# Moving the `wo` loads of a decode kernel behind its last K tile, with contiguous rows for the other weights

## Chip, cores, metric

The kernel runs on one core of a Trainium2 chip. The metric is the device time of one execution in microseconds (us), which includes about 1.8 us around the span that the profile shows.

## The reference, cut to what matters

One decode step for 8 sequences (B = 8, one token each, D = 512): grouped attention over a window of 2048 cached tokens (8 KV heads of 128, 32 query heads), the output projection `wo`, then a small MLP with `w3` (512 × 1792) and `w4` (1792 × 512). The token shift branch (`w1`, `w2`) is identically zero at sequence length 1.

```python
q = (layernorm(x) @ wq)                       # wq 512 x 4096, 4.19 MB
p = softmax(q k[-2048:] / sqrt(128)); o = p v  # K and V: 64 tiles each of 2048 x 128 bf16, 67.1 MB
h = x + o @ wo                                 # wo 4096 x 512, 4.19 MB
xb = layernorm(h)
h2 = gelu(layernorm(xb) @ w3) @ w4             # w3, w4: 1.84 MB each
out = h + xb + h2
```

Everything is bf16 and each byte is used once per step, so loading 79.2 MB is most of the work.

## The kernel before

An item i is one (sequence, KV head) pair, i = 0 to 63; a batch is the 8 items of one sequence. For each K tile the TensorE makes 16 transposes (`pe_T`) and 4 score matmuls. After each batch come softmax and 128 P·V matmuls, with V tiles of 512 KB. All loads are issued from one engine.

```python
def sp_prog(e):                                # the load program, in order
    e.dma_start(x_sb, A_x)
    for kc in range(KC):                       # KC = 4
        e.dma_start(wq_v[:, kc, :], A_wq[kc*128:(kc+1)*128, :]).then_inc(sem_wq, 16)
    for i in range(NITEM):
        ...                                    # wait for a free K slot (15 of them)
        e.dma_start(knat[:, ks, :], K tile i).then_inc(sem_k[ks], 16)
        while v_next <= i - VD and v_next < V_DEFER_FROM:    # V follows K by 5; V56..63 wait
            issue_v(v_next); v_next += 1
        for _ in range(2):                     # from item 12 on: two 128 KB pieces of wo per K
            if i >= W_START and wi < len(wdmas): ...
    ...
    while v_next < NITEM: issue_v(v_next); v_next += 1       # V56..63
    e.wait_ge(sem_Thi, W34_LAST_ITEM + 1)      # w3 and w4 reuse K slots
    for dst, src, wsem in w34dmas:             # 4 pieces of w3, 14 of w4, one semaphore
        e.dma_start(dst, src).then_inc(wsem, 16)
...
def pe_attn(e):                                # the wo product
    e.wait_ge(sem_oT, NB)
    e.wait_ge(sem_wo, 16 * N_WO)
    for h in range(H): ...                     # 32 matmuls, 4 column tiles
...
def pe_h3(e):                                  # the w3 product
    e.wait_ge(sem_w34, 16 * N_W34)
    for fc in range(FC):                       # FC = 14
        for kc in range(KC):
            e.matmul(misc[...], w3_sb[:, kc, fc*128:(fc+1)*128], uT[:, kc*B:(kc+1)*B], ...)
...
def pe_h2(e): ...                              # the w4 product, 14 matmuls
```

## Time and profile before

| | before |
|---|---|
| time, first measurement | 214.96 us (214.67 to 216.75, 3 runs) |
| span of the profiled run | 213.3 us |
| last landings: wq, K63, V63, wo, w3/w4 | 13.5, 178.2, 188.3, 89.5, 197.5 us |
| wo product, w3 product | 193.9 to 197.5, 204.0 to 205.6 us |

The landing times here and below are read from the trace: the moment when the semaphore of a load got its sixteenth increment.

These are rows of the page's slices for the kernel before, each digit or number one fortieth of the span (5.3 us): TensorE busy tenths, granted TensorE clock in tenths, busy tenths of the DMA engines, and GB/s.

```profile
...
PE   1049955998389956799769987798899589788143
...
PEclk9999999967859696795998599769966995785855
DMA  6999999999999999999999999999999999996000
GB/s 198 420 422 416 420 415 420 406 411 411 403 416 409 406 408 409 415 415 418 420 416 421 415 415 423 416 416 418 416 416 421 416 419 418 414 398 206 0 3 2
...
```

The DMA row is full and the GB/s flat from the second slice to the end of the loads. The TensorE row has holes. So the stream of bytes is the limit, and the TensorE waits for it. The waits say the same; this is the line of the view of who waited for whom, with us in total, times and the longest:

```profile
...
PE kT_ps L397 <- DMA knat<-in_A_k_cache_dram: 25.6, 28, 2.0
...
```

The chain that ended last, in order of time (start, us, what), for the kernel before:

```profile
...
156.76 16.51 DMA knat<-in_A_k_cache_dram
...
173.32 1.07 PE kT_ps L397 x16
...
193.88 3.62 PE S_ps L587 x32
...
203.96 1.67 PE misc L671 x56
...
```

The last load that this chain names is K60, which landed at 173.3 us. No load of a weight stands after it: `wo` had landed 104 us before its use, and `w3`/`w4` 6.5 us before theirs. The timeline (start, us, engine, line, what, count, and in brackets what ended the idle time before) shows the end of the kernel as a string of dependent steps:

```profile
...
188.71 1.74 PE L535 MATMUL misc<-pT_sb,vnat 128*128 128x4 bf16 x64 [0.44 <-DVE pT_sb L494]
...
190.96 1.86 PE L535 MATMUL misc<-pT_sb,vnat 128*128 128x4 bf16 x64
...
193.88 3.58 PE L587 MATMUL S_ps<-wbig,oT_all 128*8 128x512 bf16 x32 [1.06 <-DVE oT_all L549]
...
198.26 0.38 PE L604 MATMUL misc<-C_sb,sel_b 128*8 128x512 bf16 x1 [0.80 <-DVE C_sb L597]
...
198.57 0.37 PE L605 MATMUL misc<-x_sb,ident_b 8*8 8x512 bf16 x1
...
203.96 1.66 PE L671 MATMUL misc<-uT,knat 128*128 128x8 bf16 x56 [0.41 <-DVE uT L660]
...
207.57 1.87 PE L716 MATMUL S_ps<-knat,gT 128*8 128x512 bf16 x14 [1.95 <-DVE gT L705]
...
```

L535 is P·V of the last batch, L587 the wo product, L604 and L605 the two matmuls that sum it, L671 the w3 product, L716 the w4 product. The groups by shape give the w3 product and its weight loads (busy us, mean ns of one):

```profile
...
L671 PE MATMUL misc<-uT,knat 128*128 128x8 bf16 x56 | 1.7, 168 | 0.4 <-DVE uT L660 0.4
L671 PEld LDWEIGHTS misc<-uT,knat 128*128 128x128 bf16 x56 | 1.6, 104 | 0.5 <-DVE uT L660 0.5
...
```

And the view of stretches gives the granted clock (column PEclk) between the wo and w3 products, and in the w3 product:

```profile
...
core 0: us, PE busy (x) PEld busy (x) DVE busy (x) ACT busy (x) POOL busy (x), PEclk, DMA share, GB/s
...
197.60:203.20 5.60, 0.68 (x2) 0.16 (x2) 3.93 (x10) 1.30 (x3) 0.00 (x0) 0.79 0.00 0
203.90:205.70 1.80, 1.66 (x56) 1.57 (x56) 0.05 (x2) 0.00 (x0) 0.00 (x0) 0.50 0.03 9
...
```

### The profile page before, as it was taken

The numbers are of one execution on the slowest core, as the hardware profiler recorded it, in microseconds if no ns is written. First come the engines' busy times: TensorE is split into PE (matmuls) and PEld (weight loads), VectorE is DVE, ScalarE is ACT, GpSimd is POOL, SyncE is SP. The second block draws the span as 40 slices with busy tenths as digits, with TensorE's granted clock in tenths as the row PEclk, the third lists the DMA queues.
The fourth block names the chain that finished last, engine by engine and source line by source line (L and its number), as shares of the span: only waits on it lengthen the run. The fifth ranks groups of instructions, "written<-read, shape, count | busy, mean of one in ns | idle before, by whom it ended". The sixth has DMA issues, their size and how long they took to land.

```text
span 213.3 us, 6096 instructions
## 1 busy us (share of the span) xinstructions
PE 160.1 (75%) x2627; PEld 119.7 (56%) x2627; DVE 88.9 (42%) x205; ACT 81.5 (38%) x98; POOL 2.8 (1%) x11
## 2 busy tenths in 40 slices
PE   1049955998389956799769987798899589788143
PEld 0049734786267734487548764776687368563030
DVE  6104534532425332534453456147533553441652
ACT  3204748314352333413551365047515541340120
POOL 5000000000000000000000000000000000000000
PEclk9999999967859696795998599769966995785855
DMA  6999999999999999999999999999999999996000
GB/s 198 420 422 416 420 415 420 406 411 411 403 416 409 406 408 409 415 415 418 420 416 421 415 415 423 416 416 418 416 416 421 416 419 418 414 398 206 0 3 2
DMA packets 26265, 79.57 MB, mean 373 GB/s; under 512 B 2928, under 2 KB 8832, under 8 KB 25728
## 3 DMA queue, kind: packets, MB, share of 16 engines
q1 hardware_dynamic: 26240, 79.20, 92.6%
q8 instruction: 21, 0.34, 0.6%
q14 instruction: 4, 0.03, 0.0%
HBM read 79.18 MB, written 0.01 MB: 371 GB/s over the span
## 4 chain that ended last, share of the span: by engine, by line
DMA 40%; SPq 34%; PE 17%; DVE 5%; issue 3%; ACT 1%; DVEq 0%
DMA knat<-in_A_k_cache_dram 40%; SPq L247 13%; SPq L237 12%; SPq L259 8%; PE kT_ps L397 6%; PE misc L535 5%; PE S_ps L587 2%; PE S_ps L427 1%; SPq L228 1%; PE S_ps L716 1%; PE misc L671 1%; PE b L516 1%; DVE st L279 1%; DVE xb_f L292 0%; ACT P_sb L448 0%
## 5 line engine op out<-in xcount | busy, mean ns | idle before, releaser
L397 PE MATMUL kT_ps<-ident_b,knat 128*128 128x128 bf16 x1024 | 85.5, 251 | 25.7 <-DMA knat<-in_A_k_cache_dram 25.6
L408 ACT ACTIVATE kT_sb<-kT_ps 128x1024 bf16<-128x1024 bf16 x64 | 65.5, 1024 | 94.2 <-PE kT_ps L397 94.1
L397 PEld LDWEIGHTS kT_ps<-ident_b,knat 128*128 128x128 bf16 x1024 | 73.4, 114 | 43.2 <-DMA knat<-in_A_k_cache_dram 35.6
L415 DVE COPY kT_sb<-kT_ps 128x1024 bf16<-128x1024 bf16 x64 | 44.3, 692 | 69.0 <-PE kT_ps L397 68.5
L535 PE MATMUL misc<-pT_sb,vnat 128*128 128x4 bf16 x1024 | 28.7, 165 | 1.5 <-issue 1.1
L535 PEld LDWEIGHTS misc<-pT_sb,vnat 128*128 128x128 bf16 x1024 | 27.3, 98 | 4.5 <-issue 3.0
L427 PE MATMUL S_ps<-kT_sb,qblk 128*32 128x512 bf16 x256 | 29.5, 445 | 0.3 <-DVE kT_sb L415 0.3
L427 PEld LDWEIGHTS S_ps<-kT_sb,qblk 128*32 128x32 bf16 x256 | 6.7, 95 | 9.4 <-issue 4.0
L448 ACT ACTIVATE P_sb<-S_ps,negmcol 128x512 bf16<-128x512 f32 x8 | 5.5, 688 | 7.7 <-DVE negmcol L440 7.6
L369 PE MATMUL S_ps<-xlnT,wbig 128*128 128x8 bf16 x128 | 3.6, 168 | 6.1 <-DMA wbig<-in_A_wq_dram 6.1
L521 DVE COPY w_sb<-b 128x128 f32<-128x128 f32 x8 | 2.3, 292 | 13.5 <-PE b L516 13.5
L545 DVE TENSOR_TENSOR prod_sb<-misc,w_sb 128x128 f32<-128x128 f32 x8 | 2.3, 292 | 13.0 <-PE misc L535 13.0
L369 PEld LDWEIGHTS S_ps<-xlnT,wbig 128*128 128x128 bf16 x128 | 3.5, 104 | 6.2 <-issue 6.2
L438 DVE TENSOR_REDUCE mcol<-S_ps 128x1 f32<-128x512 f32 x8 | 5.5, 682 | 0.6 <-PE S_ps L427 0.6
L285 ACT ACTIVATE stdv<-mv,eps_t 8x1 f32<-8x1 f32 x3 | 0.9, 294 | 12.5 <-DVE mv L281 12.5
L385 DVE TENSOR_SCALAR qblk<-S_ps 128x32 bf16<-128x32 f32 x8 | 0.9, 182 | 9.5 <-PE S_ps L369 9.5
L587 PE MATMUL S_ps<-wbig,oT_all 128*8 128x512 bf16 x32 | 3.6, 627 | 1.1 <-DVE oT_all L549 1.1
L455 PE MATMUL misc<-ident_f,mcol 128*1 128x128 f32 x16 | 3.6, 309 | 1.0 <-DVE negmcol L440 1.0
L472 ACT ACTIVATE a_row<-d_row 1x128 f32<-1x128 f32 x8 | 2.5, 306 | 4.7 <-DVE d_row L465 4.6
L516 PE MATMUL b<-w_row,ones_row 1*128 1x128 f32 x16 | 4.0, 334 | 0.0
L285 ACT ACT_TABLE_LOAD x2 | 2.6, 1283 | 2.8 <-DVE mv L281 2.8
L494 DVE COPY pT_sb<-b 128x512 bf16<-128x512 bf16 x8 | 3.4, 426 | 0.4 <-PE b L482 0.2
(74 smaller groups left out, 66.0 us busy)
## 6 DMA issues: line engine op xcount, KB each, us to landing
knat<-in_A_k_cache_dram SPq DMA_DIRECT2D x64, 512.0 KB, 14.9
vnat<-in_A_v_cache_dram SPq DMA_DIRECT2D x64, 512.0 KB, 14.9
wbig<-in_A_wq_dram SPq DMA_DIRECT2D x4, 1024.0 KB, 8.0
wbig<-in_A_wo_dram SPq DMA_DIRECT2D x32, 128.0 KB, 9.8
knat<-in_B_w_dram SPq DMA_DIRECT2D x4, 448.0 KB, 12.8
knat<-in_B_w_dram SPq DMA_DIRECT2D x14, 128.0 KB, 6.0
x_sb<-in_A_x_dram SPq DMA_DIRECT2D x1, 8.0 KB
out_dram<-out_sb SPq DMA_DIRECT2D x1, 8.0 KB
```

The lines of the kernel that those rows point to most:

```text
L237: e.dma_start(vnat[:, vs, :].rearrange("p (c d) -> p c d", c=NC), A_v_cache[b, g, W0:SK, :].rearrange("(p c) d -> p c d", c=NC),).then_inc ...
L247: e.dma_start(knat[:, ks, :].rearrange("p (c d) -> p c d", c=NC), A_k_cache[b, g, W0:SK, :].rearrange("(p c) d -> p c d", c=NC),).then_inc ...
L259: e.dma_start(dst, src).then_inc(wsem, 16)
L369: ins = e.matmul(S_ps[:, 0, h * B:(h + 1) * B], wq_v[:, kc, h * DH:(h + 1) * DH], xlnT[:, kc * B:(kc + 1) * B], start=(kc == 0), stop=(kc ...
L397: ins = e.matmul(buf[:, c * 128:(c + 1) * 128], knat[:, ks, c * DH:(c + 1) * DH], ident_b[:, :], is_transpose=True)
L408: e.activation(kT_sb[:, i % NKT, 0:W // 2], kT_ps[i % 2][:, 0:W // 2], ACT.Copy).then_inc(sem_Elo, 1)
L415: e.tensor_copy(kT_sb[:, i % NKT, W // 2:W], kT_ps[i % 2][:, W // 2:W]).then_inc(sem_Ehi, 1)
L427: ins = e.matmul(S_ps[32 * q:32 * (q + 1), b % 2, :], qblk[:, b, g, :], kT_sb[:, i % NKT, 512 * q:512 * (q + 1)], start=(g == 0), stop=(g ...
L438: ins = e.tensor_reduce(mcol[:, j:j + 1], S_ps[:, j, :], AX.X, ALU.max)
L516: e.matmul(b6[:, WBC], ones_row[0:1, :], w_row[0:1, (b % 2) * 128:(b % 2 + 1) * 128], start=True, stop=True).then_inc(sem_wbc, 1)
L535: ins = e.matmul(misc[:, OT4.start + q * H + R * g:OT4.start + q * H + R * (g + 1)], vnat[:, vs, c * DH:(c + 1) * DH], pT_sb[:, b % 2, c, ...
L587: ins = e.matmul(S_ps[32 * j:32 * j + B, 1, :], oT_all[:, h, :], wo_v[:, h, :], start=(h < 4), stop=(h >= H - 4), tile_position=(0, 32 * j ...
```

## The change

The intent: nothing but `wq`, K and V ahead of the last K tile, since the last K starts the long end chain. `wo` moves behind K: half of it before the last four V tiles, half after; then `w3`, then `w4` in two pieces. Each piece has a semaphore of its own. And `wq`, `w3` and `w4` are laid out so that each partition reads one contiguous run of memory: `"(p k) n"` instead of `"(k p) n"`. For `w4` this renames the hidden index to f = 14p + c, so the w3 product must pick its columns with a step of 14 elements. `wo` keeps its 1 KB rows.

```diff
-            for kc in range(KC):
-                e.dma_start(wq_v[:, kc, :], A_wq[kc * 128:(kc + 1) * 128, :]).then_inc(sem_wq, 16)
+            e.dma_start(wq_v, A_wq.rearrange("(p k) n -> p k n", k=KC)).then_inc(sem_wq, 16)
 ... in the loop over K tiles:
-                for _ in range(2):
-                    if i >= W_START and wi < len(wdmas):
-                        ... one 128 KB piece of wo
 ... behind the last K tile:
             while v_next < NITEM:
+                if NITEM - v_next == G // 2:
+                    while wo_next < WO_PARTS // 2:      # WO_PARTS = 4, 1 MB each
+                        issue_wo(wo_next)
+                        wo_next += 1
                 issue_v(v_next)
                 v_next += 1
+            while wo_next < WO_PARTS:
+                issue_wo(wo_next)
+                wo_next += 1
 ...
-            for dst, src, wsem in w34dmas:
-                e.dma_start(dst, src).then_inc(wsem, 16)
+            e.dma_start(w3_sb, B_w3.rearrange("(p k) f -> p k f", k=KC)).then_inc(sem_w3, 16)
+            w4_rows = B_w4.rearrange("(p c) n -> p c n", c=FC)
+            for j in range(W4_PARTS):                   # W4_PARTS = 2
+                f0 = j * W4_F
+                e.dma_start(w4_sb[:, f0:f0 + W4_F, :],
+                            w4_rows[:, f0:f0 + W4_F, :]).then_inc(sem_w4[j], 16)
 ... pe_attn:
+                if h % WO_H == 0:
+                    e.wait_ge(sem_wo[h // WO_H], 16)
 ... pe_h3:
-            e.wait_ge(sem_w34, 16 * N_W34)
+            e.wait_ge(sem_w3, 16)
-                                   w3_sb[:, kc, fc * 128:(fc + 1) * 128],
+                                   w3_sb[:, kc, :].rearrange("p (q c) -> p c q", c=FC)[:, fc, :],
 ... pe_h2:
+                if fc % W4_F == 0:
+                    e.wait_ge(sem_w4[fc // W4_F], 16)
```

The transposes of x and u pick their columns with a step of 4 to match (cut here).

More of the change, by code (lines that the diff above doesn't have):

```diff
@@ L140, in bass_sequential_preLN__sliding_block_cached__mixer_s_mlp__decode_kernel @@
         sem_wq = S("sem_wq")
-        sem_w34 = S("sem_w34")
-        sem_wo = S("sem_wo")
+        sem_w3 = S("sem_w3")
+        sem_w4 = [S(f"sem_w4_{i}") for i in range(2)]
+        sem_wo = [S(f"sem_wo{i}") for i in range(4)]
         sem_out = S("sem_out")
@@ L209, in pool_prog @@
             e.memset(oT_all[:], 0.0).then_inc(sem_pool, 1)
-        wdmas = []
-        for h in range(H):
-            wdmas.append((wo_v[:, h, :], A_wo[h * 128:(h + 1) * 128, :], sem_wo))
-        w34dmas = []
-        for kc in range(KC):
-            w34dmas.append((w3_sb[:, kc, :], B_w3[kc * 128:(kc + 1) * 128, :], sem_w34))
-        for fc in range(FC):
-            w34dmas.append((w4_sb[:, fc, :], B_w4[fc * 128:(fc + 1) * 128, :], sem_w34))
-        N_WO = H
-        N_W34 = KC + FC
-        W_START = 12
+        WO_PARTS = 4
+        WO_H = H // WO_PARTS
+        W4_PARTS = 2
+        W4_F = FC // W4_PARTS
         V_DEFER_FROM = max(NITEM - G, 0)
@@ L226, in sp_prog @@
             e.dma_start(x_sb[:], A_x.rearrange("b s d -> (b s) d")).then_inc(sem_x, 16)
-            for kc in range(KC):
-                e.dma_start(wq_v[:, kc, :], A_wq[kc * 128:(kc + 1) * 128, :]).then_inc(sem_wq, 16)
-            wi = 0
+            e.dma_start(wq_v, A_wq.rearrange("(p k) n -> p k n", k=KC)).then_inc(sem_wq, 16)
             v_next = 0
@@ L253, in sp_prog, with issue_wo @@
                     v_next += 1
-                for _ in range(2):
-                    if i >= W_START and wi < len(wdmas):
-                        if wi == 0:
-                            e.wait_ge(sem_dveP, DVEP_QBLK)
-                        dst, src, wsem = wdmas[wi]
-                        e.dma_start(dst, src).then_inc(wsem, 16)
-                        wi += 1
-            while wi < len(wdmas):
-                if wi == 0:
-                    e.wait_ge(sem_dveP, DVEP_QBLK)
-                dst, src, wsem = wdmas[wi]
-                e.dma_start(dst, src).then_inc(wsem, 16)
-                wi += 1
+            def issue_wo(j):
+                h0 = j * WO_H
+                e.dma_start(wo_v[:, h0:h0 + WO_H, :],
+                            A_wo[h0 * 128:(h0 + WO_H) * 128, :].rearrange(
+                                "(h p) n -> p h n", p=128)).then_inc(sem_wo[j], 16)
+            e.wait_ge(sem_dveP, DVEP_QBLK)
+            wo_next = 0
             while v_next < NITEM:
+                if NITEM - v_next == G // 2:
+                    while wo_next < WO_PARTS // 2:
+                        issue_wo(wo_next)
+                        wo_next += 1
                 issue_v(v_next)
                 v_next += 1
+            while wo_next < WO_PARTS:
+                issue_wo(wo_next)
+                wo_next += 1
             if W34_LAST_ITEM >= 0:
                 e.wait_ge(sem_Thi, W34_LAST_ITEM + 1)
-            for dst, src, wsem in w34dmas:
-                e.dma_start(dst, src).then_inc(wsem, 16)
+            e.dma_start(w3_sb, B_w3.rearrange("(p k) f -> p k f", k=KC)).then_inc(sem_w3, 16)
[4 more added lines that the diff above has]
+                            w4_rows[:, f0:f0 + W4_F, :]).then_inc(sem_w4[j], 16)
             e.wait_ge(sem_dveP, DVEP_OUT_READY)
@@ L348, in pe_pro1 @@
             for kc in range(KC):
-                ins = e.matmul(pT_ps[:, kc * B:(kc + 1) * B], xln_b[:, kc * 128:(kc + 1) * 128],
+                ins = e.matmul(pT_ps[:, kc * B:(kc + 1) * B], xln_b[:, :].rearrange("b (p k) -> b k p", k=KC)[:, kc, :],
                                ident_b[0:B, 0:B], is_transpose=True)
@@ L364, in pe_q @@
             e.wait_ge(sem_dveP, DVEP_XLNT)
-            e.wait_ge(sem_wq, 16 * KC)
+            e.wait_ge(sem_wq, 16)
             ins = None
@@ L582, in pe_attn @@
             e.wait_ge(sem_oT, NB)
-            e.wait_ge(sem_wo, 16 * N_WO)
             ins = None
             for h in range(H):
+                if h % WO_H == 0:
+                    e.wait_ge(sem_wo[h // WO_H], 16)
                 j = h % 4
@@ L650, in pe_uT @@
             for kc in range(KC):
-                ins = e.matmul(pT_ps[:, kc * B:(kc + 1) * B], u_b[:, kc * 128:(kc + 1) * 128],
+                ins = e.matmul(pT_ps[:, kc * B:(kc + 1) * B], u_b[:, :].rearrange("b (p k) -> b k p", k=KC)[:, kc, :],
                                ident_b[0:B, 0:B], is_transpose=True)
```

## The prediction

> **What bounds the kernel now.** The slices' DMA row stands at 403 to 423 GB/s from 5 to 190 us: until the last load the kernel is a 79.2 MB stream. The trace's landing times show who waits: from K tile 7 on, most transposes start 0.05 us after their K tile lands, and where the TensorE falls behind (after each P·V block) it catches up within the batch. K lands every 2.49 us where only K and V flow, every 3.18 us while two 128 KB pieces of wo sit between (K13 to K28, 43 to 91 us). The last K (63) lands at 178.2, the last V at 188.3, the last of w3/w4 at 197.5. The end is a dependent chain (timeline): K63 transposes end 184.5, P·V 188.7 to 192.8, wo product 193.9 to 197.5, w3 product 204.0 to 205.6, w4 product 207.6 to 209.4, end 213.3. w3/w4 land 6.5 us before use, wo over 100 us before. So wo's bytes ahead of K63 delay everything, while loads behind K63 hide under the end chain.
>
> **What changes, costed.**
> 1. wo leaves the K stream: 16 intervals × (3.18 − 2.49) = −11.0 us; K63 lands near 167.2. Later stretches already run at 2.49 us per K without the TensorE losing ground; I expect the early one to do so too. All critical, up to the last P·V (start about 177.7).
> 2. The tail becomes DMA-paced. After K63 come V56–59 (to 172.4), half of wo (at its pace of 0.34 us per 128 KB: to 177.9), V60–63 (1.24 us each: to 182.8), wo parts 3 and 4 (185.6, 188.3), w3 (192.7), w4 (197). P·V could end at 181.8 but waits for V63: 183.3. The wo product could end at 188.0, but its last quarter lands at 188.3: it ends 189.2. Given back: 2.7 of the 11.0.
> 3. Then the chain is as before (15.8 us after the wo product). w3 is wanted at about 195.7, w4 at 199: both landed. Splitting them is a safeguard, not a gain.
> 4. Contiguous rows: w4 from 1 to 7 KB, wq from 8 to 32 KB. wq already streams at about 420 GB/s; w4 perhaps 0.3 us, behind slack. wo keeps 1 KB rows.
> 5. Cost: with f = 14p + c the w3 product loads weight columns with a step of 28 bytes. [...] no trace here has such a load. The 56 pairs take 1.66 us (30 ns each). My estimate is +1 us, from 0 to +4, fully critical.
>
> **Sum.** 214.96 − 11.0 + 2.7 + 1.0 [...] ≈ 207.3 us. Range 204.5 to 210.5. Chances: faster by over 2% 0.90, within 2% 0.09, slower 0.01.
>
> **What would show each step.** (1) K63 landing near 167, K spaced 2.5 us from 25 us on, DMA row unchanged. (2) TensorE waits for V loads in the last P·V and for wo in its product; V63 near 183, last wo near 188. (3) No wait on w3 or w4. (5) The w3 product's weight loads and length against 1.66 us.
>
> **What would make it wrong.** TensorE falls behind early once it loses the slack of the wo pieces, or its granted clock drops sooner, so K63's transposes end later than 173.6. The strided weight load costs several us. wo in 1 MB pieces of 1 KB rows runs slower than 385 GB/s with no K/V between. The single 4 MB wq load lands later than 13.5 us.

The reason given for the cost of a 28-byte step was shown by no trace; the +1 us is the author's estimate. And the sum came to 207.3 us with a fourth term, −0.4 us for a faster granted clock after the new waits; no trace showed that, so the term is cut. The three terms left come to 207.7 us (214.96 − 11.0 + 2.7 + 1.0). The range and the predicted span of 205.6 us below are those of the whole sum.

## The result

The kernel after takes 209.17 us (208.15 to 209.39, 4 runs) against 215.86 us (214.67 to 217.06, 4 runs) of before. The ratio is 0.9687, with a 95% interval of 0.9627 to 0.9748: faster, by 3.1%. The span of the profiled run fell from 213.3 to 207.3 us.

| us | before | predicted | after |
|---|---|---|---|
| wq landed | 13.5 | 13.5 | 13.7 |
| K63 landed | 178.2 | 167.2 | 167.1 |
| V63 landed | 188.3 | 182.8 | 182.6 |
| last of wo landed | 89.5 | 188.3 | 188.1 |
| w3, last of w4 landed | 197.5 together | 192.7, 197 | 192.4, 196.6 |
| wo product ended | 197.5 | 189.2 | 189.2 |
| length of the w3 product | 1.66 | 2.7 | 3.56 |
| span | 213.3 | 205.6 (213.3 − 7.7) | 207.3 |

The same rows of the slices, for the kernel after:

```profile
...
PE   1039985999589869977999697969986996764263
...
PEclk9999998888998899787979997999796969655555
DMA  6989999999999999999999999999999999999500
GB/s 204 468 368 417 421 417 419 414 420 419 413 419 416 417 421 417 417 417 417 419 415 415 422 419 417 412 420 418 418 417 415 422 399 371 400 389 418 225 3 2
...
```

The stream is as full as before and ends only 0.9 us earlier (196.6 against 197.5 us). What moved is what is in it. The waits for loads, for the kernel after:

```profile
...
PE kT_ps L396 <- DMA knat<-in_A_k_cache_dram: 19.6, 23, 2.0
...
PE misc L534 <- DMA vnat<-in_A_v_cache_dram: 1.5, 3, 0.7
...
PE S_ps L587 <- DMA wbig<-in_A_wo_dram: 1.2, 1, 1.2
...
```

The wait for K fell by 6.0 us (25.6 to 19.6), and two waits are new: for V in the last P·V and for `wo` in its product. No line names `w3` or `w4`. The end of the chain for the kernel after:

```profile
...
175.03 13.09 DMA wbig<-in_A_wo_dram
...
188.17 1.06 PE S_ps L587 x6
...
196.11 3.56 PE misc L671 x56
...
```

The chain's last load is now a piece of `wo`, landing at 188.1 us, in the place of K60. The w3 product behind it takes 3.56 us where it took 1.67. In the timeline of the kernel after:

```profile
...
181.41 0.59 PE L534 MATMUL misc<-pT_sb,vnat 128*128 128x4 bf16 x16 [0.66 <-DMA vnat<-in_A_v_cache_dram]
...
182.63 0.59 PE L534 MATMUL misc<-pT_sb,vnat 128*128 128x4 bf16 x16 [0.63 <-DMA vnat<-in_A_v_cache_dram]
...
184.27 2.73 PE L587 MATMUL S_ps<-wbig,oT_all 128*8 128x512 bf16 x24 [1.06 <-DVE oT_all L548]
...
188.17 1.03 PE L587 MATMUL S_ps<-wbig,oT_all 128*8 128x512 bf16 x8 [1.17 <-DMA wbig<-in_A_wo_dram]
...
189.99 0.59 PE L604 MATMUL misc<-C_sb,sel_b 128*8 128x512 bf16 x1 [0.80 <-DVE C_sb L597]
...
190.51 0.58 PE L605 MATMUL misc<-x_sb,ident_b 8*8 8x512 bf16 x1
...
```

P·V waits for each of its last two V tiles (0.66 and 0.63 us), the wo product stops 1.17 us for its last quarter, and the two sums take 0.59 and 0.58 us instead of 0.38 and 0.37. The w3 product and its weight loads by shape, and the stretches that answer to those of before:

```profile
...
L671 PE MATMUL misc<-uT,knat 128*128 128x8 bf16 x56 | 3.5, 202 | 0.4 <-DVE uT L660 0.4
L671 PEld LDWEIGHTS misc<-uT,knat 128*128 128x128 bf16 x56 | 3.5, 166 | 0.5 <-DVE uT L660 0.5
...
```

```profile
...
189.30:195.40 6.10, 1.10 (x2) 0.16 (x2) 4.01 (x10) 1.35 (x3) 0.00 (x0) 0.50 0.83 348
196.10:199.70 3.60, 3.54 (x56) 3.46 (x56) 0.01 (x1) 0.00 (x0) 0.00 (x0) 0.50 0.02 5
...
```

The granted clock between the products was 0.50, where it was 0.79 before; in the w3 product it was 0.50 in both kernels, so the clock is not what made that product longer. (The records of these two traces know only 1.00 and 0.50; 0.79 is a mean, of 1.00 up to 200.8 us and 0.50 from there on.)

### The profile page after: what moved, and what is told of

Same layout as the page of the kernel before. It is cut to its first block, busy times and chain, and to the rows that moved or that the text cites. A ratio compares the mean times of both kernels' runs of the same rounds, so it can differ in the third digit from the quotient of the medians.

```text
span 207.3 us, 6052 instructions
## 1 busy us (share of the span) xinstructions
PE 157.3 (76%) x2627; PEld 117.2 (57%) x2627; DVE 88.8 (43%) x205; ACT 81.4 (39%) x98; POOL 2.8 (1%) x11
## 4 chain that ended last, share of the span: by engine, by line
DMA 50%; SPq 27%; PE 16%; DVE 4%; issue 1%; ACT 0%; DVEq 0%
DMA knat<-in_A_k_cache_dram 44%; SPq L229 14%; PE kT_ps L396 8%; SPq L239 7%; DMA wbig<-in_A_wo_dram 6%; SPq L249 6%; PE misc L671 2%; PE misc L534 2%; PE S_ps L426 2%; PE S_ps L718 1%; DVE st L278 1%; PE S_ps L587 1%; PE misc L454 0%; DVE xb_f L291 0%; DVE C_sb L728 0%
## 5 line engine op out<-in xcount | busy, mean ns | idle before, releaser
L396 PE MATMUL kT_ps<-ident_b,knat 128*128 128x128 bf16 x1024 | 81.1, 243 | 19.7 <-DMA knat<-in_A_k_cache_dram 19.6
L396 PEld LDWEIGHTS kT_ps<-ident_b,knat 128*128 128x128 bf16 x1024 | 69.2, 110 | 36.4 <-DMA knat<-in_A_k_cache_dram 29.0
L426 PE MATMUL S_ps<-kT_sb,qblk 128*32 128x512 bf16 x256 | 28.5, 430 | 0.3 <-DVE kT_sb L414 0.3
L671 PE MATMUL misc<-uT,knat 128*128 128x8 bf16 x56 | 3.5, 202 | 0.4 <-DVE uT L660 0.4
L671 PEld LDWEIGHTS misc<-uT,knat 128*128 128x128 bf16 x56 | 3.5, 166 | 0.5 <-DVE uT L660 0.5
```

Source lines behind the costliest of these rows:

```text
L396: ins = e.matmul(buf[:, c * 128:(c + 1) * 128], knat[:, ks, c * DH:(c + 1) * DH], ident_b[:, :], is_transpose=True)
L426: ins = e.matmul(S_ps[32 * q:32 * (q + 1), b % 2, :], qblk[:, b, g, :], kT_sb[:, i % NKT, 512 * q:512 * (q + 1)], start=(g == 0), stop=(g ...
L671: ins = e.matmul(misc[:, H3.start + fc * B:H3.start + (fc + 1) * B], w3_sb[:, kc, :].rearrange("p (q c) -> p c q", c=FC)[:, fc, :], uT[:, ...
```

## The experiments

Twelve kernels ran, in three sets of four; each set ran on a chip of its own together with 11 runs of the kernel before. Times of one set compare directly; across sets I compare ratios to the kernel before. The kernel before spreads over 214.3 to 217.2 us, 2.4 to 2.6 us within each chip, more than any of the other kernels does; I did not look for the cause, and it makes the ratios uncertain by about 0.4%. Executions of the other kernels differ too (`cols1`: three at 206.4 to 206.6 us, three at 207.3 to 207.4), so the span of one profiled run decides nothing below about 0.9 us; there I go by the medians or by the length of a single step in the trace. Clear of 2%, all kernels are faster than before, except `layout_only` (the same) and `wo_half_early` (unclear). The theory: (A) the gain is the order of the loads alone, (B) the tail is then paced by the last byte of `wo`, (C) the step of the weight columns is a pure cost in the w3 product. The rivals stand in each expectation.

### Set 1: the layout and the order, apart

`cols1` puts the w3 columns side by side again, with w4 in 1 KB rows:

```diff
-                                   w3_sb[:, kc, :].rearrange("p (q c) -> p c q", c=FC)[:, fc, :],
+                                   w3_sb[:, kc, fc * 128:(fc + 1) * 128],
 ... and for w4
-            w4_rows = B_w4.rearrange("(p c) n -> p c n", c=FC)
-                            w4_rows[:, f0:f0 + W4_F, :]).then_inc(sem_w4[j], 16)
+                            B_w4[f0*128:(f0+W4_F)*128, :].rearrange("(c p) n -> p c n", p=128)).then_inc(sem_w4[j], 16)
```

> The kernel after, with w3's weight columns contiguous again (f = 128c + p) and w4 therefore in 1 KB rows. Theory: the 28-byte step alone makes the w3 product 3.54 us instead of 1.66; here it returns to 1.7 us and the span falls by 1.9 us, from 207.3 to 205.4. w4 then lands about 0.4 us later (197.0) and is still not waited for. Rival (the w4 load in flight or the clock slows the w3 product): it stays near 3.5 us and the span near 207.3.

`cols2` and `cols7` keep some contiguity: groups of 2 or 7 neighbouring rows of w4 per partition, so a column step of 4 or 14 bytes.

```diff
+                                   w3_sb[:, kc, fc // 2 * 256:(fc // 2 + 1) * 256].rearrange("p (q c) -> p c q", c=2)[:, fc % 2, :],   # cols2
+                            B_w4[f0*128:f1*128, :].rearrange("(g p c) n -> p g (c n)", p=128, c=2)).then_inc(sem_w4[j], 16)
 ... cols7: the same with 7, (p c) n, one group in each of the two w4 pieces
```

Each of the next two expectations names two outcomes. The second for `cols2`, 3.5 us, is that any step other than one element costs as much as the 28-byte step did.

> Groups of 2: weight columns at a step of 4 bytes, w4 in 2 KB rows. [...] the w3 product takes 1.7 us and the span is as in cols1, 205.4. [...] it takes about 3.5 us and the span is 207.3.

> Groups of 7: a step of 14 bytes, w4 in 7 KB rows. [...] the w3 product takes 3.3 to 3.5 us and the span is 207.0 to 207.3. If the cost grows evenly with the step, it takes about 2.6 us.

`order_only` has the order and the separate waits of the change, and the layouts of before (wq and w3 in four loads each, w4 as in `cols1`):

```diff
-            e.dma_start(wq_v, A_wq.rearrange("(p k) n -> p k n", k=KC)).then_inc(sem_wq, 16)
+            for kc in range(KC):
+                e.dma_start(wq_v[:, kc, :], A_wq[kc * 128:(kc + 1) * 128, :]).then_inc(sem_wq, 16)
 ... w3 likewise; w4, w3 columns as in cols1
```

> Only the load order and the separate waits of the change; wq, w3 and w4 in the row layout of before. Theory: the order is the whole gain and the layout a net cost of 1.9 us, so the span is 205.5, faster than the kernel after, with K63 landing at 167.1. Rival (contiguous rows stream faster and carry part of the gain): wq or w3/w4 land over 1 us later and the span is 208 or more.

| | step of w3 columns | w3 product's weight loads, busy | span | median time | ratio to before (95%) |
|---|---|---|---|---|---|
| cols1 | 2 bytes | 1.6 us | 205.4 | 206.93 | 0.959 (0.955 to 0.963) |
| cols2 | 4 bytes | 1.6 us | 205.6 | 206.92 | 0.959 (0.955 to 0.963) |
| cols7 | 14 bytes | 3.1 us | 207.1 | 208.85 | 0.968 (0.964 to 0.972) |
| after (set of its own) | 28 bytes | 3.5 us | 207.3 | 209.17 | 0.969 (0.963 to 0.975) |
| order_only | 2 bytes | 1.6 us | 205.5 | 207.26 | 0.960 (0.956 to 0.964) |

The deciding lines, groups by shape, of `cols1`, of `cols2` and of `cols7`:

```profile
...
L670 PEld LDWEIGHTS misc<-uT,knat 128*128 128x128 bf16 x56 | 1.6, 104 | 0.5 <-DVE uT L659 0.5
...
```

```profile
...
L670 PEld LDWEIGHTS misc<-uT,knat 128*128 128x128 bf16 x56 | 1.6, 104 | 0.5 <-DVE uT L659 0.5
...
```

```profile
...
L670 PEld LDWEIGHTS misc<-uT,knat 128*128 128x128 bf16 x56 | 3.1, 154 | 0.5 <-DVE uT L659 0.5
...
```

The step is the cause of the longer w3 product. The row length of `w4` and its landing differ in these kernels too, but `cols7` has the same 7 KB rows as the kernel after, and in `layout_only` below all of `w4` had landed 7.5 us before the product, whose weight loads still took 3.5 us: a load in flight is not the cause. A step of 4 bytes is free (weight loads of 1.6 us, as at 2 bytes), one of 14 makes the product 1.5 us longer, one of 28 1.9 us. That is neither what "any step but one" asked for (3.5 us at 4 bytes) nor what "evenly with the step" did (2.6 us at 14 bytes). No run tries a step between 4 and 14 bytes, and why the cost sets in between them was not shown. The 28-byte layout costs the kernel after 1.9 us of span (207.3 − 205.4), and the order together with the separate waits gives the whole gain: `order_only` is as fast as `cols1` within the spread, with K63 landing at 167.2 us. This run does not part the two. The earlier K63 is the work of the order, since no K tile waits for a weight's semaphore; the separate wait for `w4` is measured by `w34_one` below; what the four semaphores of `wo` are worth no run shows (an estimate from the traces: with one for all, the whole product of 3.6 us would start at 188.1 us and end at 191.7, not at 189.2). The rival that contiguous rows carry part of the gain falls: wq landed at 13.3 us in four loads (`order_only`) and at 13.3 to 13.7 in one (all other kernels with the change's `wq` load). Only w4 gained: its last piece landed at 197.1 in `cols1` (1 KB rows), 0.5 us later than in the kernel after, and 2.6 us before its product started at 199.7.

### Set 2: the layout alone, and the three waits of the tail

`layout_only` is the kernel before with the row layouts of the change and nothing else moved:

```diff
-            for kc in range(KC):
-                e.dma_start(wq_v[:, kc, :], A_wq[kc * 128:(kc + 1) * 128, :]).then_inc(sem_wq, 16)
+            e.dma_start(wq_v, A_wq.rearrange("(p k) n -> p k n", k=KC)).then_inc(sem_wq, 16)
 ... w3 and w4 as in the change, still one semaphore; wo unmoved
```

> The kernel before with only the row layouts of the change (wq in one load, w3, w4 contiguous per partition); wo still among the early K tiles, one wait for w3 and w4. Theory: nothing is gained in the stream, and the w3 product takes 3.5 us, so the time is 1.9 us above before (ratio 1.005 to 1.013). Rival (the row layout carries part of the gain): faster than before, K63 landing over 1 us before 178.2.

Measured: 217.78 us, ratio 1.0115 (1.0069 to 1.0161), span 215.7. It is slower than before, by a little more than expected, though not by 2%. K63 landed at 178.1 us, as before. Its w3 weight loads, by shape:

```profile
...
L670 PEld LDWEIGHTS misc<-uT,knat 128*128 128x128 bf16 x56 | 3.5, 167 | 0.5 <-DVE uT L659 0.5
...
```

So the layout taken alone loses. In its profiled run P·V also ran a little later than in the kernel before (it ended 0.7 us later; the transposes of K63, for one, took 1.56 us where they took 1.32). Of that 0.6 us was left when the w3 product started; with the 1.9 us of the product it makes up the 2.4 us of span.

`wo_last` puts all V tiles ahead of any `wo`:

```diff
-                if NITEM - v_next == G // 2:
+                if False:
```

> The kernel after with all V tiles before any of wo. Theory: the last byte of wo paces the tail, not V63. V63 lands at 177.4 instead of 182.6 and P.V no longer waits (it ends near 181.2 instead of 183.2), but the last quarter of wo lands at 188.1 as before, so the wo product ends at 189.2 and the span stays 207.3 (within 0.3). Rival (the wait for V63 is what was given back): the span falls by 1.5 to 2 us.

Measured: 209.11 us, ratio 0.9702 (0.9665 to 0.9739), span 207.2: unchanged, as theory B says. The timeline of its end:

```profile
...
180.75 1.87 PE L534 MATMUL misc<-pT_sb,vnat 128*128 128x4 bf16 x64
...
183.68 2.73 PE L587 MATMUL S_ps<-wbig,oT_all 128*8 128x512 bf16 x24 [1.06 <-DVE oT_all L548]
...
188.13 1.03 PE L587 MATMUL S_ps<-wbig,oT_all 128*8 128x512 bf16 x8 [1.73 <-DMA wbig<-in_A_wo_dram]
...
```

P·V runs through without a wait (it ends at 182.6 and not at the expected 181.2, since the TensorE came to it later than in the kernel after), the wo product starts earlier, and stops for the last quarter of `wo` all the same, to end at 189.2. The waits for V of the kernel after cost it nothing.

`wo_three` leaves out the load of the last quarter of `wo` (a wrong result):

```diff
-            while wo_next < WO_PARTS:
+            while wo_next < WO_PARTS - 1:
 ... the last 8 heads read wo_v[:, h % (H - WO_H), :] and wait for nothing
```

> The kernel after without the load of the last quarter of wo (its product reads another quarter, so the result is wrong on purpose). Theory: the wo product then runs without a wait from 184.3 to 188.0 instead of ending at 189.2, and the span falls by 1.1 us to 206.2; w3 and w4 land 2.7 us earlier and nobody notices. If wo's last landing were not critical, the span stays 207.3.

Measured: 207.45 us, ratio 0.9636 (0.9593 to 0.9679), span 205.6. The timeline:

```profile
...
184.72 3.25 PE L587 MATMUL S_ps<-wbig,oT_all 128*8 128x512 bf16 x32 [1.06 <-DVE oT_all L548]
...
188.77 0.38 PE L604 MATMUL misc<-C_sb,sel_b 128*8 128x512 bf16 x1 [0.81 <-DVE C_sb L597]
...
```

The wo product ran through from 184.7 to 188.0, so it ended 1.2 us earlier. Most of the other 0.5 us came from the two sums: they took 0.38 and 0.37 us here, as in the kernel before at a granted clock of 1.00, and 0.59 and 0.58 in the kernel after at 0.50. The last landing of `wo` is critical, and 1 MB of it is worth only about 1.2 us (1.7 with the sums), because the TensorE stands right behind it.

`w34_one` makes the w3 product wait for w4 too, as the one semaphore of before did:

```diff
             e.wait_ge(sem_w3, 16)
+            for s4 in sem_w4:
+                e.wait_ge(s4, 16)
```

> The kernel after with the w3 product waiting for w4 too, as the single semaphore of before did. w4 lands at 196.6 and the w3 product started at 196.1: it is held by 0.5 to 0.6 us, span 207.8. Predicted on record: the separate waits are a safeguard, worth nothing; if w4 were really in hand there, the span stays 207.3.

Measured: 210.02 us, ratio 0.9752 (0.9717 to 0.9787), span 208.0. In the same set `wo_last`, which stands at the time of the kernel after, took 209.11. The wait in the view of waits:

```profile
...
PE misc L673 <- DMA knat<-in_B_w_dram: 1.9, 1, 1.9
...
```

Of these 1.9 us of idle time about 0.4 us (the step before, in every kernel) would be there anyway. The rest is 1.5 us; the profiled run got about 0.85 us of it back: the last quarter of its wo product took 0.60 us and not 1.03 (379 ns for one matmul and not 610), and the two sums 0.42 us less.

```profile
...
188.25 0.60 PE L587 MATMUL S_ps<-wbig,oT_all 128*8 128x512 bf16 x8 [1.15 <-DMA wbig<-in_A_wo_dram]
...
189.65 0.38 PE L604 MATMUL misc<-C_sb,sel_b 128*8 128x512 bf16 x1 [0.80 <-DVE C_sb L597]
...
```

So the separate semaphore for w4 is worth about 0.9 us by the medians. My prediction called it worth nothing.

### Set 3: the dose, and a better version

`wo_half_early` puts half of `wo` back into the K stream:

```diff
+                if i in (20, 28):
+                    e.wait_ge(sem_dveP, DVEP_QBLK)
+                    issue_wo((20, 28).index(i))
 ... behind the last K only parts 2 and 3 are left
```

> The kernel after with the first half of wo back in the K stream (two 1 MB loads, behind K20 and K28); half the dose of before. Theory: K63 lands 5.5 us later, 172.6 instead of 167.1, the last P.V ends near 187 and the wo product (no wait for wo: the last quarter lands at 188.1 still, before it is wanted) near 191.7, so the span is about 209.8 to 210.2. Rival (only the landing of the last byte of wo counts, wherever wo stands): the span stays 207.3.

Measured: 212.38 us, ratio 0.9823 (0.9785 to 0.9860), span 209.6. K63 landed at 172.6 us, half way between 167.1 and 178.2. `wo` had landed at 188.1 as in the kernel after, but now that was early enough:

```profile
...
188.31 3.58 PE L589 MATMUL S_ps<-wbig,oT_all 128*8 128x512 bf16 x32 [1.06 <-DVE oT_all L550]
...
```

The wait before the product is for its other operand, the attention output (DVE oT_all). So each quarter of `wo` (1 MB) ahead of the last K delays K63 by 2.8 us (11.1 / 4 and 5.5 / 2), and the tail turns from "paced by wo" to "paced by K63" between none and half of `wo` early.

`cols1_fine`, `cols2_fine` and `cols2_fine_last` combine the cheap column step with smaller last pieces of `wo`:

```diff
-        WO_PARTS = 4
-        WO_H = H // WO_PARTS
+        WO_H = [8, 8, 8, 4, 2, 2]
+        WO_AT = [sum(WO_H[:j]) for j in range(len(WO_H))]
-                if h % WO_H == 0:
-                    e.wait_ge(sem_wo[h // WO_H], 16)
+                if h in WO_AT:
+                    e.wait_ge(sem_wo[WO_AT.index(h)], 16)
 ... w3 columns and w4 as in cols1 / cols2; _last: V ahead of wo as in wo_last
```

In the first, the rival is that the small last pieces of `wo` land later; the reason that it gave was not shown.

> Contiguous w3 columns, and wo in pieces of 8, 8, 8, 4, 2, 2 heads. Theory: after the last landing (188.1) only two matmuls are left instead of eight, so the wo product ends near 188.5 instead of 189.2 and the span is 204.7 against 205.4 of the contiguous columns alone. Rival [...]: 205.4 or more.

> As the one before, with w4 in 2 KB rows and weight columns at a step of 4 bytes: w3 product 1.7 us, span 204.7, the same as with step 2 bytes since w4 is in hand by then.

> As the one before, with all V ahead of wo. V63 is no longer waited for, but wo's last piece still lands near 188.1: the same span within 0.3 us, 204.7.

Measured: 206.24 us (ratio 0.9547, 0.9511 to 0.9582), 206.47 us (0.9557, 0.9524 to 0.9589) and 206.95 us (0.9575, 0.9543 to 0.9607), spans 205.4, 205.1 and 205.3. All three beat the kernel before and the kernel after, but the intervals overlap those of `cols1` and `cols2` (0.959), so the smaller pieces are not shown to give anything, and the 0.7 us that I expected of them did not come in the spans. The end of the wo product of `cols1_fine`:

```profile
...
184.34 2.73 PE L587 MATMUL S_ps<-wbig,oT_all 128*8 128x512 bf16 x24 [1.06 <-DVE oT_all L548]
...
187.28 1.91 PE L587 MATMUL S_ps<-wbig,oT_all 128*8 128x512 bf16 x8 [0.21 <-DMA wbig<-in_A_wo_dram]
...
```

Two reasons can be read there. The last piece landed at 188.55 instead of 188.13. And the two matmuls left behind it need 0.6 us (in the kernel after, at a granted clock of 0.50, a matmul of this shape takes 0.62 us on average; there four, in different column tiles, start within 0.02 us, and the next four 0.38 to 0.43 us later), not the quarter of 1.03 us that I had reckoned. So this product ends at 189.2 as before.

## Why the prediction was right, and where it missed

The direction, the main mechanism and the range were right: 207.3 us predicted (204.5 to 210.5), 209.17 measured. As a change of span it is −7.7 us predicted and −6.0 measured; the missing 1.7 us are terms 5 and 6, and term 3 was wrong as well. Point by point:

1. "wo leaves the K stream: 16 intervals × (3.18 − 2.49) = −11.0 us; K63 lands near 167.2." Measured −11.1 and 167.1. `order_only` shows that the order does it, `wo_half_early` that half a dose gives half.
2. "The tail becomes DMA-paced … Given back: 2.7 of the 11.0." Measured 2.8: the wo product ended 8.3 us earlier. The pacing by the last byte of `wo`, not by V63, is shown by `wo_last` and `wo_three`. My text listed the wait for V as the first loss, but it is hidden behind the other.
3. "Splitting them is a safeguard, not a gain." Wrong: `w34_one` is about 0.9 us slower than its neighbour. The numbers already held it: w4 at about 197, and the w3 product wanting to start at 195.7. I compared w4 only with the w4 product and forgot that the single semaphore of before would have made w3 wait for it.
4. Contiguous rows: "wq already streams at about 420 GB/s; w4 perhaps 0.3 us, behind slack". Measured nothing for wq, and 0.5 us for w4 behind 2.6 us of slack.
5. "My estimate is +1 us, from 0 to +4, fully critical." That the step costs time was right, the term was mis-sized: +1.9 us, shown by `cols1` and by the layout alone. The traces give the size (weight loads of 1.6 us at 4 bytes, as at 2, 3.1 us at 14, 3.5 us at 28, with nothing tried between 4 and 14); the reason for it was not shown.
6. The term of −0.4 us for a faster clock. It was an estimate without working, and it was wrong in sign: the clock granted between the products was 0.50 and not 0.79, so the two sums took 0.42 us more (0.59 + 0.58 against 0.38 + 0.37).

On term 6: in the traces of the kernels before and after, the clock records know only 1.00 and 0.50, and change only at multiples of one step of 3.41 us. The steps do not fall at the same times in the two. In the kernel before, the wo product filled the step from 193.98 to 197.40 us (3.41 us of busy matmul), and the clock in the next was 1.00. In the kernel after, the wait of 1.17 us for the last quarter of `wo` falls inside the step from 184.81 to 188.22 us (2.25 us of busy matmul), and the clock in the next was 0.50. This table has the waits for `wo` inside the wo product and the length of the two sums for every kernel, from the timelines:

| run | waits for `wo` in the product, us | the two sums, us |
|---|---|---|
| before, `layout_only`, `wo_three`, `wo_half_early` | none | 0.38, 0.37 |
| `w34_one` | 1.15 | 0.38, 0.37 |
| `cols1`, `cols2`, `order_only`, after, `cols7`, `wo_last` | 1.07, 1.08, 1.17, 1.17, 1.20, 1.73 | 0.59, 0.58 |
| `cols1_fine` | 0.21 | 0.59, 0.58 |
| `cols2_fine_last` | 0.76 and 0.28 | 0.59, 0.58 |
| `cols2_fine` | none listed (product 4.36 us long) | 0.59, 0.58 |

Five kernels have the fast sums, nine the slow ones. The wait alone does not settle it: `w34_one` waited 1.15 us and the kernel after 1.17, and the first had fast sums, the second slow ones. What decides the granted clock was not shown; no run was made to test it.

The two misses in size, 0.9 us in term 5 and 0.8 us in term 6, make up the 1.7 us between the predicted span (205.6) and the measured one (207.3).

## What to carry to other kernels

When a kernel is limited by its stream of bytes and ends in a long dependent chain, order the loads by what starts that chain: bytes not needed before it cost their full time ahead of it (here 11.1 us for the 4.19 MB of `wo`), and behind it only as much as they outlast the chain's own steps (here 2.8 us). A layout that makes a load contiguous pays only where that load is waited for, and it may hand its step to a compute operand (here 28 bytes, for 1.9 us): check the step of the weight columns in bytes before trading it for longer rows. Give each piece of a weight that a separate step uses its own semaphore (here about 0.9 us for that of `w4`), and compare its landing with the step that would otherwise wait.

## What else the traces show

- The step of weight columns: 56 loads of 128 × 128 bf16 took 1.6 us at steps of 2 and 4 bytes, 3.1 us at 14 bytes and 3.5 us at 28 bytes, all at a granted clock of 0.50. At 28 bytes that is a factor of 2.2 (3.46 us busy in the kernel after against 1.57 in the kernel before).
- The length of rows: in the kernel after, pieces with 1 KB rows landed more slowly than pieces with longer ones. A 1 MB piece of `wo` took 2.69 and 2.73 us between landings at 1 KB rows (390 and 384 GB/s), a 0.92 MB piece of `w4` 2.12 and 2.14 us at 7 KB rows (433 and 429 GB/s).
- The granted clock: it also fell while matmuls stood on record without a gap. Of the 22 falls from 1.00 to 0.50 in the traces of the kernels before and after, 13 came after a step of 3.41 us in which matmul was busy 95% or more. After one of them, at 176.9 us in the kernel before, the transposes of K61 and K62 took 1.87 and 1.89 us against 1.07 for K60. Nor did a busy record always bring the clock back: in `layout_only` the w3 product (8 columns moving per matmul) was busy for 3.40 us from 204.6 to 208.0 us at a clock of 0.50, and the w4 product behind it took 1.9 us, as in the kernel before at 0.50 (1.87 us); behind the wo product (512 columns) of the kernel before the clock was 1.00. What decides it was not shown.
- The 16 increments of a load: the first and the last stood under 1 us apart at the first four K tiles (0.43 to 0.50 us in the kernel before, 0.81 to 0.89 in the kernel after) and 4.4 us apart at K63, in both kernels; the kernel's waits are for the last. The cause was not tested.
